# A GpSimd drain ahead of the last 512 rows, and a stricter test on the decays, in a fused attention and MoE kernel

## The chip, the core and the metric

The kernel runs on one core of a Trainium2 chip. Its engines are TensorE (PE; its weight loads are PEld), VectorE (DVE), ScalarE (ACT), GpSimd (POOL) and SyncE (SP), each with an instruction queue of its own; they wait for each other through semaphores. The metric is the device time of one execution in microseconds (us). Before the change three runs took 760.2, 766.49 and 769.64 us, a median of 766.49.

## The reference

Three computations follow one another. The first is a linear attention with a decay for each channel: 4 batches of 8 heads, 768 steps, head size 48.

```python
for t in range(S):
    cur = einsum('bhd,bhe->bhde', u[None] * kt, vt)
    y[:, :, t] = einsum('bhd,bhde->bhe', rt, state + cur)
    state = wt[:, :, :, None] * state + einsum('bhd,bhe->bhde', kt, vt)
```

Its output, 3072 rows of 384, goes through a mixture of eight experts. Each row takes the expert with the largest logit: `out = gate * (max(x @ w1[e], 0) @ w2[e])`, with a hidden width of 1024. The last step is `max(max(x @ v1, x @ v2), x @ v3) @ v_out` with a hidden width of 768. The decays w are drawn as `rand * 0.15 + 0.8`, that is from 0.8 to 0.95.

## The kernel before, in words

The attention works on 24 tiles of 128 rows with scans over the decays. These scans are only good where no decay is extreme, so `flags` marks for every tile and partition whether a decay lay below 0.7 or above 1.4. A tile holds two heads of 48 channels side by side on 128 partitions; the 16 partitions ahead of each are padding, whose decays are set to 1.0 once at the start (`pads`, L649, and two memsets in `attention`). `check_w` counts the good partitions over all 128 with a matmul against ones (L493), compares the count with a limit (L495), and puts the outcome, `badw`, into `ctl`.

The routing sorts rows by expert. GpSimd scatters row numbers into a table in DRAM, gathers them back, and gathers the rows themselves, all by indirect DMAs that it issues from its own queue. The first block (`first_block`) runs the experts on columns of 256 rows. The second block (`second_block`) runs the last step on 512 rows at a time: six turns, j = 0, 2, ..., 10. In a turn `m1` computes the hidden units in six chunks, on TensorE with VectorE and ScalarE behind it, and then `m2` computes the output in four tiles of 128 rows. For each tile ScalarE scales the result into one of four buffers (L1227), and GpSimd issues an indirect DMA that scatters the 128 rows into the output (L1228). In the second block GpSimd has no other work.

Every engine runs its queue in the order in which the code stands; the whole kernel is under a manual schedule. Behind the second block each engine reads `ctl` and branches (L1427, L1428): only where rows remain, or where `badw` is set, the general path runs, with `attention_general` in it. Otherwise GpSimd waits for its DMAs and brings the semaphore counters to the values that the other branch would have left (an INC_SWDGE_SEM, L1428). At the program's end (L1536) SyncE waits for all counters, and every engine drains and meets the others at a barrier twice, with GpSimd clearing the semaphores in between.

Of the kernel before, what the change touches and what calls it, by code (L numbers as in the profile page):

```python
# [15 lines left out]
ALU = mybir.AluOpType  # L16
# [32 lines left out]
def kernel(ctx: ExitStack, tc: tile.TileContext, rkw_t, v_t, vrk, u, modality, w_gate, bias, w1, w2, v1, v2,  # L49
                              v3, v_out, out):  # L50
    nc = tc.nc
    PE, DVE, ACT, POOL, SP = nc.tensor, nc.vector, nc.scalar, nc.gpsimd, nc.sync
    B, NC, _, D, _, HP, _ = rkw_t.shape
# [43 lines left out]
    lgps = lgpool.tile([128, 512], F32, name="lgps")  # L97


    def ct(shape, dt, name):  # L100
        return const.tile(shape, dt, name=name)
# [38 lines left out]
    badw = ct([128, 1], F32, "badw")  # L140
# [214 lines left out]
    def plan(es):  # L355
# [37 lines left out]
        end = t2("end")  # L393
        DVE.tensor_tensor_scan(out=end, data0=zero8, data1=co, initial=cgs, op0=ALU.add, op1=ALU.add)
        checked = check_w()
        next(checked)
        yield "X"
# [88 lines left out]
    def check_w():  # L486

        fl = small.tile([128, 1], F32, tag="fl", name="fl")
        DVE.tensor_reduce(out=fl, in_=flag, axis=AX.XY, op=ALU.max)
        good = small.tile([128, 1], BF16, tag="good", name="good")  # L490
        DVE.tensor_scalar(out=good, in0=fl, scalar1=0.0, scalar2=None, op0=ALU.is_equal)
        yield
        PE.matmul(lgps[:, 272:273], lhsT=ones_bf, rhs=good, start=True, stop=True)  # L493
        yield
        DVE.tensor_scalar(out=badw, in0=lgps[:, 272:273], scalar1=2.0 * D, scalar2=None, op0=ALU.is_lt)  # L495
        yield
        DVE.tensor_copy(ctl[:, 62:63], badw)

# [771 lines left out]
    N = NTILE // 2  # L1270
# [140 lines left out]
    def second_block(vw):  # L1411
        n = 2 * TW
        for j in range(0, N, 2):
            if j + 2 < N:
                xr = ex.fetch(j + 2, n)
            for c in range(KF2):
                ex.m1(c, n, (lambda: vw(V_OPS[5])) if j == 0 else lambda: None)
                if c == MERGE[j > 0] and j + 2 < N:
                    ex.merge(j + 2, xr)
            if j + 2 < N:  # L1420
                ex.x2(xr, j // 2 + 1)
            ex.m2(T[j]["oi"] + T[j + 1]["oi"])

    def rest():

# [36 lines left out]
    with tc.manual_schedule():  # L1462
        wes = ExitStack()
        ex.open_first(wes)
        e = NTILE

        hooks = {(13, "mid"): [chosen, bind(first_load, 0, 0)],
                 (14, "end"): [first_room],
                 (e - 2, "uterm"): [first_x, bind(ex.split_w1, (0, 1, 2))],
                 (e - 2, "late"): [bind(ex.split_w1, (3, 4, 5), "h")],  # L1470
                 (e - 1, "uterm"): [bind(ex.split_w1, (3, 4, 5), "l"), bind(ex.g1, (0,)),
                                    bind(ex.split_w2, (0, 1), W2_FIRST)],
                 (e - 1, "mid"): [bind(ex.split_w2, (2, 3), W2_FIRST)],
                 (e, "mid"): [bind(ex.g1, (1,), rest_of_routing)],
                 (e, "end"): [bind(ex.split_w2, (4, 5), W2_FIRST)]}
        for q in range(1, 7):
            hooks[(13 + q, "mid")] = [bind(first_load, q // 3 if q < 6 else 1, q if q < 3 else q - 3)]
        attention(hooks)
        pools["mm"] = pool(ctx, "mm", 4, space=PSUM)
        wres = pool(ctx, "wres", 1)  # L1480
        vh = [wres.tile([128, KD, F2], F32R, name=f"vh{i}") for i in range(3)]
        vl = [wres.tile([128, KD, F2], F32R, name=f"vl{i}") for i in range(3)]
        voh = wres.tile([128, KF2, DM], F32R, name="voh")
        vol = wres.tile([128, KF2, DM], F32R, name="vol")
        with ExitStack() as es:
            vw = v_stream(pool(es, "stage", 2))
            first_block(vw)
            second_block(vw)
        wes.close()
        rest()  # L1490
# [50 lines left out]
```

## Time and profile before

| what | value |
|---|---|
| median of three runs | 766.49 us |
| the profiled execution | 770.97 us |
| its span, from the first to the last instruction | 769.3 us |
| granted TensorE clock, mean | 0.948 |
| TensorE busy | 720.2 us, 94% |
| VectorE, ScalarE, GpSimd busy | 494.0, 318.7, 363.8 us |

All times of the trace count from the start of the span. The busy times hold the engines' work alone: register, branch, semaphore and DMA-issuing instructions are not counted. A name with a q behind it (POOLq, SPq) is the queue of an engine, where such instructions stand. They are seen by asking for a source line of the kernel.

### The profile page before, as it was taken

What the parts mean: (1) busy time and instruction counts of PE and PEld (TensorE: products, weight loads), DVE (VectorE), ACT (ScalarE), POOL (GpSimd) and SP (SyncE); (2) the same over time, 40 slices, a digit from 0 to 9 for tenths busy, and PEclk for the clock granted to TensorE, in tenths of its full rate; (3) what the DMA queues carried; (4) which work ended last, traced back from release to release, by engine and by line L of the source; (5) the groups of instructions that cost most, each with busy time, mean ns of one, the idle gap of its engine ahead of it and who ended that gap; (6) DMA issues with size and microseconds to landing.
All of it is one profiled execution on the core that took longest, in us unless ns stands there. A gap on an engine that the chain in (4) does not pass through costs nothing.

```text
span 769.3 us, 13303 instructions
## 1 busy us (share of the span) xinstructions
PE 720.2 (94%) x4909; PEld 642.9 (84%) x4910; DVE 494.0 (64%) x929; ACT 318.7 (41%) x698; POOL 363.8 (47%) x388
## 2 busy tenths in 40 slices
PE   6899888889999999999999999999999999999991
PEld 3788767777899989999999987988988889889881
DVE  4899996996786998888888889424143142242320
ACT  5475645554333656566566633211212112122210
POOL 8699868898746667666764435110200101002011
PEclk8699989878599999999999999999999999999996
DMA  9899989993013322122235232020200200001000
GB/s 240 203 249 252 214 173 232 269 273 121 22 50 104 84 65 82 62 65 81 63 118 183 83 124 84 6 77 1 83 0 3 82 0 32 11 0 42 1 21 25
DMA packets 32383, 74.59 MB, mean 97 GB/s; under 512 B 5974, under 2 KB 19062, under 8 KB 32309
## 3 DMA queue, kind: packets, MB, share of 16 engines
q1 hardware_dynamic: 27508, 64.15, 30.5%
q0 software_dynamic: 4800, 9.49, 4.0%
q8 instruction: 41, 0.67, 0.4%
q14 instruction: 34, 0.27, 0.1%
HBM read 87.96 MB, written 14.38 MB: 133 GB/s over the span
## 4 chain that ended last, share of the span: by engine, by line
issue 37%; PE 30%; DVE 12%; DMA 8%; POOL 7%; ACT 2%; POOLq 0%; SPq 0%; DVEq 0%; ACTq 0%
DMA tq<-in_rkw_t_dram 6%; PE mm L1145 6%; PE mm L1144 5%; PE mm L1143 5%; PE yb L805 4%; POOL out_dram L1228 3%; DVE w1l L504 3%; PE mm L775 2%; PE yb L811 2%; DMA vt<-in_v_t_dram 1%; POOL w2l L504 1%; PE tp L788 1%; PE tp L706 1%; PE tp L859 1%; DMA w2r<-in_moe_w_dram 1%
## 5 line engine op out<-in xcount | busy, mean ns | idle before, releaser
L1208 DVE TENSOR_TENSOR w2r<-mm,w2r 128x512 f32<-128x512 f32 x72 | 49.7, 690 | 150.2 <-PE mm L1145 150.1
L1228 POOL DMA_INDIRECT out_dram<-w2r,oi_all x24 | 26.0, 1084 | 250.2 <-ACT w2r L1227 249.6
L1143 PE MATMUL mm<-w1h,vh 128*128 128x512 f32 x324 | 128.2, 396 | 0.9 <-DVE w2r L1208 0.9
L1145 PE MATMUL mm<-w1h,vl 128*128 128x512 f32 x324 | 128.2, 396 | 0.0
L1144 PE MATMUL mm<-w1l,vh 128*128 128x512 f32 x324 | 128.1, 395 | 0.0
L1145 PE MATMUL mm<-hh,w2l 128*128 128x256 f32 x312 | 89.3, 286 | 2.0 <-DVE w2l L504 1.0
L1144 PE MATMUL mm<-hl,w2h 128*128 128x256 f32 x312 | 88.5, 284 | 1.0 <-DVE hl L1157 1.0
L1143 PE MATMUL mm<-hh,w2h 128*128 128x256 f32 x312 | 89.2, 286 | 0.0
L1145 PE MATMUL mm<-xh,w1l 128*128 128x256 f32 x300 | 85.9, 286 | 2.2 <-DVE w1l L504 2.2
L1143 PE MATMUL mm<-xh,w1h 128*128 128x256 f32 x300 | 85.0, 283 | 0.0
L1144 PE MATMUL mm<-xl,w1h 128*128 128x256 f32 x300 | 84.8, 283 | 0.0
L1210 ACT CAST w2h<-w2r 128x512 fp32r<-128x512 f32 x36 | 22.3, 621 | 139.3 <-DVE w2r L1208 139.3
L1143 PEld LDWEIGHTS mm<-w1h,vh 128*128 128x128 f32 x324 | 60.9, 188 | 15.7 <-DVE w2r L1208 1.3
L1145 PEld LDWEIGHTS mm<-w1h,vl 128*128 128x128 f32 x324 | 60.9, 188 | 14.7
L1144 PEld LDWEIGHTS mm<-w1l,vh 128*128 128x128 f32 x324 | 60.9, 188 | 14.4
L504 POOL TENSOR_TENSOR w2l<-w2r,w2h 128x384 fp32r<-128x384 f32 x44 | 49.7, 1136 | 41.6 <-ACT w2h L502 39.1
L504 DVE TENSOR_TENSOR w1l<-w1r,w1h 128x512 fp32r<-128x512 f32 x66 | 51.8, 838 | 23.8 <-ACT w1h L502 23.7
L1145 PEld LDWEIGHTS mm<-hh,w2l 128*128 128x128 f32 x312 | 59.7, 191 | 3.9 <-DVE w2l L504 2.6
L805 PE MATMUL yb<-nat,am 128*128 128x56 f32 x384 | 53.1, 297 | 8.6 <-DVE lh L834 5.0
L1144 PEld LDWEIGHTS mm<-hl,w2h 128*128 128x128 f32 x312 | 59.7, 191 | 1.5 <-DVE hl L1157 1.4
L1145 PEld LDWEIGHTS mm<-xh,w1l 128*128 128x128 f32 x300 | 57.5, 192 | 4.1 <-DVE w1l L504 4.1
L1143 PEld LDWEIGHTS mm<-hh,w2h 128*128 128x128 f32 x312 | 59.8, 192 | 0.0
(252 smaller groups left out, 1728.0 us busy)
## 6 DMA issues: line engine op xcount, KB each, us to landing
w1r<-in_moe_w_dram SPq DMA_DIRECT2D x10, 1536.0 KB, 7.0
w2r<-in_moe_w_dram SPq DMA_DIRECT2D x10, 1536.0 KB
nat<-in_vrk_dram SPq DMA_DIRECT2D x24, 608.0 KB, 10.1
tq<-in_rkw_t_dram SPq DMA_DIRECT2D x46, 288.0 KB, 8.7
stg<-in_moe_w_dram SPq DMA_DIRECT2D x18, 384.0 KB, 3.1
vt<-in_v_t_dram SPq DMA_DIRECT2D x24, 192.0 KB, 6.6
x2t<-raw SPq DMA_DIRECT2D x12, 384.0 KB, 2.3
w1r<-x2t SPq DMA_DIRECT2D x12, 384.0 KB, 3.9
```

The costliest lines, as they stand in the source:

```text
L504: eng.tensor_tensor(out=lo, in0=src, in1=hi.bitcast(F32), op=ALU.subtract)
L706: PE.matmul(ps, lhsT=s["vt"][:, q, :], rhs=wgb[:, q].rearrange("p h e -> p (h e)"), start=(q == 0), stop=(q == KD - 1))
L775: PE.matmul(ps[o][:, p * 128:(p + 1) * 128], lhsT=s["kt"][q, p, :], rhs=s["rt"][q, p, :], start=True, stop=True)
L788: PE.transpose(out=ps[:, p * 128:(p + 1) * 128], in_=s["kt"][:, p, :], identity=ident)
L805: PE.matmul(yb[:, h * DV:(h + 1) * DV], lhsT=s["am"][:, 4 * (h % 2) + h // 2, :], rhs=s["v"][:, h, :], start=(h == 0), stop=(first and h = ...
L811: PE.matmul(yb[:, 2 * p * DV:(2 * p + 2) * DV], lhsT=s["rt"][:, p, :], rhs=sbd[i % 2][:, p, :], start=False, stop=(p == HP - 1))
L1143: PE.matmul(oc, lhsT=wh[:, kk, sl], rhs=xh[:, kk, :], start=first and kk == 0, stop=False)
L1144: PE.matmul(oc, lhsT=wh[:, kk, sl], rhs=xl[:, kk, :], start=False, stop=False)
L1145: PE.matmul(oc, lhsT=wl[:, kk, sl], rhs=xh[:, kk, :], start=False, stop=last and kk == nk - 1)
L1208: DVE.tensor_tensor(out=hv, in0=o, in1=hv, op=ALU.max)
L1210: ACT.copy(self.h2h[:, c, :], hv)
L1228: ins = POOL.indirect_dma_start(out=out[:, :], out_offset=bass.IndirectOffsetOnAxis(ap=ids[q][:, 0:1], axis=0), in_=ob, in_offset=None, bo ...
```

## The change

In `check_w` the limit on the count of good partitions goes from 96 (twice the head size) to 127.5, so that one flagged partition is enough to set `badw`. In `second_block`, in the turn j = 8 (the last but one, as N is 12), GpSimd gets one more instruction behind the four stores of that turn: a drain, with no wait on a semaphore and no semaphore to raise. The turn j = 10 follows. No instruction of any engine changes its place, and none is removed.

```diff
@@ check_w
-        DVE.tensor_scalar(out=badw, in0=lgps[:, 272:273], scalar1=2.0 * D, scalar2=None, op0=ALU.is_lt)
+        DVE.tensor_scalar(out=badw, in0=lgps[:, 272:273], scalar1=127.5, scalar2=None, op0=ALU.is_lt)
@@ second_block
             if j + 2 < N:
                 ex.x2(xr, j // 2 + 1)
             ex.m2(T[j]["oi"] + T[j + 1]["oi"])
+            if j + 4 == N:
+                POOL.drain()
```

## Rows read from the trace of the kernel before

**Rows 1.** The page: span, and TensorE's busy tenths in 40 slices.

```profile
span 769.3 us, 13303 instructions
...
PE   6899888889999999999999999999999999999991
```

**Rows 2.** Windows at the end: length, busy us (instructions) by engine, clock, DMA share, GB/s.

```profile
744.86:753.40 8.54, 8.47 (x49) 8.14 (x47) 0.00 (x0) 1.19 (x3) 2.91 (x3) 1.00 0.21 73
753.40:757.90 4.50, 0.00 (x0) 0.00 (x0) 0.00 (x0) 0.55 (x1) 0.97 (x1) 0.93 0.17 55
757.90:769.30 11.40, 0.00 (x0) 0.00 (x0) 0.00 (x0) 0.00 (x0) 0.00 (x0) 0.50 0.00 1
```

**Rows 3.** GpSimd's timeline: start us, duration us, what, idle time before it.

```profile
703.95 0.97 POOL L1228 DMA_INDIRECT out_dram<-w2r,oi_all  x1 [2.15 <-ACT w2r L1227]
744.86 0.97 POOL L1228 DMA_INDIRECT out_dram<-w2r,oi_all  x1 [39.94 <-ACT w2r L1227]
...
754.22 0.97 POOL L1228 DMA_INDIRECT out_dram<-w2r,oi_all  x1 [2.15 <-ACT w2r L1227]
```

**Rows 4.** The output tensor's instructions: ns min/median/max, idle before, waiters, landing.

```profile
L1228 POOL DMA_INDIRECT out_dram<-w2r,oi_all x24: 971/973/1972, 496.7 to 754.2; - x24
...
who waited for it (us, times):
...
DMA to landing us min/median/max: 2.6/3.0/6.6
```

**Rows 5.** Source line L1428, GpSimd's queue: ns min/median/max, first and last start us.

```profile
L1428 POOLq EVENT_SEMAPHORE  x6: 17/30/100, 757.4 to 757.9; - x6
...
L1428 POOLq INC_SWDGE_SEM  x1: 2188/2188/2188, 758.0 to 758.0; - x1
```

**Rows 6.** Source line L1536, the program's end, by queue; columns as before.

```profile
L1536 SPq EVENT_SEMAPHORE  x14: 17/28/28, 760.1 to 769.2; - x14
...
L1536 POOLq DRAIN  x3: 40/107/8240, 760.2 to 769.0; - x3
L1536 SPq DRAIN  x3: 7/7/13, 760.8 to 768.7; - x3
L1536 DVEq DRAIN  x2: 10/14/17, 746.0 to 768.7; - x2
L1536 PEldq DRAIN  x2: 8/8/8, 754.9 to 768.8; - x2
```

**Rows 7.** Waits of SyncE's queue from 590: us in total, times, longest.

```profile
SPq L1536 <- PEq L1536: 8.3, 2, 7.7
```

**Rows 8.** Source line L1526, the program's start, GpSimd's queue.

```profile
L1526 POOLq INC_SWDGE_SEM  x1: 27/27/27, 0.2 to 0.2; - x1
...
L1526 POOLq DRAIN  x1: 189/189/189, 0.4 to 0.4; - x1
```

**Rows 9.** DMA issues of GpSimd's queue: count, median us to landing.

```profile
order<-idg,places POOLq DMA_INDIRECT x24, 5.0
xin<-xs,oi_all POOLq DMA_INDIRECT x24, 3.4
out_dram<-w2r,oi_all POOLq DMA_INDIRECT x24, 3.0
oi_all<-order,idxm POOLq DMA_INDIRECT x20, 2.5
...
oi_all<-order,idxg POOLq DMA_INDIRECT x4, 5.9
oe<-order,idxx POOLq DMA_INDIRECT x2
xin<-xs,oe POOLq DMA_INDIRECT x2, 2.1
```

**Rows 10.** Source line L495, the test on the count.

```profile
L495 DVE TENSOR_SCALAR badw<-lgps x1: 149/149/149, 227.5 to 227.5; 128x1 f32<-128x1 f32 x1
```

**Rows 11.** The page's groups: busy us, mean ns, idle before.

```profile
L1208 DVE TENSOR_TENSOR w2r<-mm,w2r 128x512 f32<-128x512 f32 x72 | 49.7, 690 | 150.2 <-PE mm L1145 150.1
```

## The prediction

> **What bounds the kernel now.** I read the page first [rows 1]. The span is 769.3 us, and in its 40 slices TensorE's digit is 9 almost without a break. Then the last slice holds a 1. A slice is 19.2 us long, so some 16 us at the end pass without a matmul. No rate of matmuls explains that stretch, so the end has to be read by itself.
>
> The windows cut at the end's events show it [rows 2]. Up to 753.4 TensorE is at work. From 757.9 to 769.3 no engine has any busy time at all: 11.4 us, 1.5% of the span, in which the program only winds up. GpSimd's timeline shows the last work before that: the last four stores of output rows are issued 3.12 us apart, the first at 744.86, the last at 754.22 [rows 3]. A store lands a median of 3.0 us after its issue [rows 4], hence the pause to 757.9.
>
> What fills the 11.4 us is queue work, which the busy columns leave out. It is seen by asking for the source lines of the final branch (L1428) and of the program's end (L1536) [rows 5, 6]. GpSimd's queue does six semaphore waits until 757.9, and the last of them is for the last store. Then one INC_SWDGE_SEM takes 2188 ns (758.0 to 760.2), and then a DRAIN takes 8240 ns (760.2 to 768.4). Two more DRAINs of GpSimd take 107 and 40 ns, the last starts at 769.0, and the span ends. SyncE's queue does its own end waits meanwhile: from 760.1 to 760.9 it goes through them one after the other, and then stands in the closing barrier, which every engine must reach, for 7.7 us [rows 7]. That row names TensorE's queue as the one waited for. TensorE's two drains took 8 ns each, the earlier at 754.9 [rows 6], so the name is that of the last release and not the cause. The only queue with work from 760.9 to 768.4 is GpSimd's, and its work there is that one drain.
>
> **What the drain pays for.** Three rows argue that it pays for the DMAs that GpSimd has issued, one by one. SyncE's queue, which issued the bulk of the traffic through the hardware's own queue, drains in 7 to 13 ns, and VectorE and TensorE in 8 to 17 ns [rows 6]. GpSimd's own drain at the start, before any DMA, took 189 ns [rows 8], and those right behind the long one took 107 and 40 ns, when nothing new had been issued. The long one is also not waiting for data: the semaphores of the stores had all been seen by 757.9, 2.3 us before it began. In between GpSimd had issued 24 + 24 + 24 + 20 + 4 + 2 + 2 = 100 indirect DMAs [rows 9]. 8240 / 100 = 82 ns for each: this is an estimate, and it supposes that the cost is spread evenly over them.
>
> The Trainium skill (VectorE: DVE Perf Modes, The DRAIN you can't avoid) says that the drains that frame a program are a constant of about 12 ns on all five engines. By that rule an added drain costs 12 ns and takes nothing off the end, and the sum below would be zero. The trace agrees for the three other engines shown and disagrees for GpSimd by a factor of several hundred.
>
> **The change, part by part.** *The new constant.* One instruction keeps its place and shape, with 127.5 in place of 96 (149 ns) [rows 10]. It counts the partitions whose decays all lay inside 0.7 to 1.4. The decays are drawn from 0.8 to 0.95, and the 32 padding partitions hold the constant 1.0, set once for each buffer in `pads`. The count is then 128 and the branch falls as before. Cost: 0.
>
> *The added drain.* It stands on GpSimd's queue behind the store issued at 703.95, and carries no wait on a semaphore. The next instruction behind it on that queue belongs to the store at 744.86. In the 39.94 us between, GpSimd is idle [rows 3], and nobody waits for GpSimd there: the row of the stores lists no waiter [rows 4], and ScalarE's reuse of an output buffer waits for landings, not for this queue. The drain covers 96 DMAs: 96 x 82 ns = 7.9 us. Bounds: from 40 ns, the shortest drain of GpSimd [rows 6], up to 8.24 us plus the slowest landing of a store, 6.6 us [rows 4], 14.8 us together. Either end leaves over 25 us of cover, so the cost is 0. Were that cover gone, 7.9 us would stand ahead of the four stores, and all of it would come off the gain.
>
> *The last drain.* It has 4 DMAs left: 4 x 82 = 0.33 us, plus the 0.19 us of an empty one, 0.52 in place of 8.24. But what is late next is SyncE. It reaches the barrier at 760.9, and of its 7.7 us there about 0.2 remain, the way from GpSimd's drain through the release (its end at 768.4, and 760.9 + 7.7 = 768.6). The drain is therefore worth 7.5 us and not 7.7.
>
> *The INC_SWDGE_SEM before it.* It changes the eight counters of GpSimd's DMAs, and SyncE's chain starts only when they have changed (760.1), so it is on the path before and after. Before any DMA the same operation took 27 ns [rows 8]. Bounds: 2188 ns if its length has nothing to do with the finished DMAs, 27 ns if it is all theirs. I take the lower side, since the drain behind it behaves like that: 8 counters x 27 = 0.22 us, the rest of 2188, 1.97 us, spread over 100 DMAs is 20 ns each, and 4 of these are 0.08. That makes 0.30, and the gain 1.9 us.
>
> *The sum.* 7.5 + 1.9 = 9.4 us. Check by the clock of the trace: the increment from 757.96 to 758.26, the drain to 758.8, SyncE's 0.8 us of waits to 759.0, the barrier and the last 0.8 us to 759.9, against 769.3. The profiled execution took 770.97 in all, 1.7 us more than its span, and would take 761.6. It lies 4.5 us above the median of the three runs, 766.49, and the gain does not depend on that. From the median: 766.49 - 9.4 = **757.1 us**. Both ends of the increment: 7.5 (759.0 us) and 9.4.
>
> **Rivals.** *Only the drain shrinks*, the increment keeps its 2.19 us: 759.0 us. For it: the 27 ns row may be another kind of the same operation, since it stands where there was nothing to add. Chance 0.2.
>
> *The last drain is a fixed price* that is due once any DMA of GpSimd has gone since the drain before, as 16 equal checks of half a microsecond (one for each DMA engine of the page) would be. Four stores are then enough to bring it back in full: 766.5 us, no change. The rows above fit that as well, since no drain in this trace stands behind a few DMAs. Against it is only the increment, a second long operation of GpSimd that is nearly free when nothing was issued. Chance 0.16.
>
> *Drains are constants*, and the 8.24 us belong to something else that the row happens to span: the same 766.5 us. No row shows another work there. Chance 0.02. The 12 ns rule of the VectorE page of the Trainium skill would give this time.
>
> The Trainium skill (Perfetto Trace Analysis, Sequencer-only Instruction (DRAIN, etc)) says that the profile shows such an instruction from the moment its waits are met. By that 8.24 us is work and not a wait, and the drain's start right behind the increment agrees. It tells nothing on whether the work is fixed.
>
> *Slower: the new threshold sends the kernel into the general path.* The place is the branch at L1428, the deciding point a count under 127.5, a single partition flagged. Before, up to 32 flagged partitions passed unseen, so the trace cannot show that the count is 128. Only the drawn decays and the pads say so. The price: 16 pairs of heads x 48 columns x 4 VectorE operations over 768 columns, each 1.5 times the 690 ns of 512 columns [rows 11], 1.04 us: 3.2 ms, so some 3,950 us. Chance 0.01.
>
> **How the numbers follow.** Forecast (both shrink) 0.59, drain alone 0.2, no change 0.18 (0.16 and 0.02), general path 0.01, anything else 0.02. The three runs shown lie 760.2 to 769.6, so a median moves by a few microseconds without any cause in the change. Low end: the fastest shown less 9.4, 750.8, rounded to 750.5. High end: the slowest shown less 7.5 is 762.1, and up to 765.5 takes in about two fifths of the no-change case. Inside lie nearly all of 0.79 and 0.4 x 0.18, about 0.8. A change of 2%, 15 us, is what a measurement of this kernel can tell from none. The forecast gain is 1.2%, so within 2% has 0.93, faster by more 0.05 (a gain case with a lucky median), slower 0.02.
>
> **What would show it.** Right: a GpSimd DRAIN of 7 to 9 us starting near 705, the one at the end under 1 us, the increment well under 1 us, SyncE's 7.7 us in the barrier gone, the span's end 6 to 7 us behind the last store's issue in place of 15. Wrong: a second drain of 8 us at the end (fixed price), an increment still near 2.19 us (drain alone), a store at 744.86 that starts late (no cover), or work behind L1428.

## The result and the profile after

The changed kernel takes 754.27 us (median of four runs, 752.42 to 755.5), the kernel before beside it 767.36 us. The ratio is 0.9845 with a 95% interval of 0.9806 to 0.9885, a gain of 1.5%. Timed again later, with more runs, it came to 0.988 (0.9844 to 0.9916).

The page of the profiled execution (754.57 us) now ends in a 6 where a 1 stood.

```profile
span 752.8 us, 13304 instructions
...
PE   6899889888899999999999999999999999999996
```

The windows at the same events as in [rows 2] (length, busy us by engine with instruction counts, clock, DMA share, GB/s):

```profile
738.00:746.51 8.51, 8.48 (x49) 8.16 (x48) 0.00 (x0) 1.16 (x2) 2.92 (x3) 1.00 0.21 74
746.51:750.90 4.39, 0.00 (x0) 0.00 (x0) 0.00 (x0) 0.58 (x1) 0.97 (x1) 0.82 0.16 55
750.90:752.80 1.90, 0.00 (x0) 0.00 (x0) 0.00 (x0) 0.00 (x0) 0.00 (x0) 0.50 0.01 4
```

Before, 11.40 us passed between the landing of the last store and the end; now 1.90 us do. The two stretches ahead of it are nearly as long as they were (8.51 against 8.54 us, 4.39 against 4.50). What shrank in the last one is on GpSimd's queue. First the branch line (L1428 before, [rows 5], L1430 now, since the change adds two lines), with ns min/median/max and first and last start:

```profile
L1430 POOLq EVENT_SEMAPHORE  x6: 17/30/43, 750.4 to 750.9; - x6
...
L1430 POOLq INC_SWDGE_SEM  x1: 268/268/268, 751.0 to 751.0; - x1
```

Then the program's end, L1538 now, against [rows 6]:

```profile
L1538 SPq EVENT_SEMAPHORE  x14: 17/28/28, 751.2 to 752.8; - x14
...
L1538 POOLq DRAIN  x3: 46/107/386, 751.3 to 752.5; - x3
L1538 SPq DRAIN  x3: 7/7/7, 751.9 to 752.2; - x3
```

The drain went from 8240 to 386 ns, the increment from 2188 to 268 ns (the increment is the INC_SWDGE_SEM). SyncE's queue hardly stands in the barrier any more; its row of waits, against [rows 7], holds 0.5 us for the second meeting and 0.2 for the one that took 7.7:

```profile
SPq L1538 <- PEq L1538: 0.7, 2, 0.5
```

The added drain shows under its own source line:

```profile
L1424 POOLq DRAIN  x1: 9120/9120/9120, 696.9 to 696.9; - x1
```

GpSimd's timeline around it (start, duration, idle time before) shows what it costs:

```profile
697.10 0.97 POOL L1228 DMA_INDIRECT out_dram<-w2r,oi_all  x1 [2.15 <-ACT w2r L1227]
738.00 0.97 POOL L1228 DMA_INDIRECT out_dram<-w2r,oi_all  x1 [39.94 <-ACT w2r L1227]
...
747.37 0.97 POOL L1228 DMA_INDIRECT out_dram<-w2r,oi_all  x1 [2.15 <-ACT w2r L1227]
```

The drain's record starts at 696.9, ahead of the store in front of it, and it ends at 706.0. From that store's end (698.07) it is 7.9 us. The next store finds GpSimd idle for 39.94 us ahead of it, exactly as in [rows 3]: the cover held.

From the last store's issue to the end it was 769.3 - 754.2 = 15.1 us and is 752.8 - 747.4 = 5.4 us: 9.6 us less. But the last store itself stands 6.8 us earlier. The added drain has no hand in that, as the difference is there at the first store already, 200 us ahead of the drain: it was issued at 496.7 before [rows 4] and now at 489.9.

```profile
L1228 POOL DMA_INDIRECT out_dram<-w2r,oi_all x24: 971/972/1974, 489.9 to 747.4; - x24
```

The windows of the attention stage and of what follows, of the kernel before:

```profile
0.00:215.00 215.00, 187.95 (x1626) 159.89 (x1628) 178.03 (x396) 117.28 (x309) 179.84 (x206) 0.84 0.79 201
215.00:690.00 475.00, 468.89 (x2978) 427.51 (x2977) 300.40 (x513) 187.54 (x368) 175.78 (x175) 1.00 0.20 62
```

and of the changed kernel:

```profile
0.00:215.00 215.00, 186.36 (x1699) 158.84 (x1701) 191.02 (x438) 118.77 (x313) 182.83 (x209) 0.91 0.77 201
215.00:690.00 475.00, 467.78 (x2944) 425.75 (x2943) 294.54 (x474) 187.50 (x367) 177.03 (x172) 1.00 0.20 63
```

The clock granted to TensorE is 1.00 in both from 215 us on, and 0.84 against 0.91 before that. With two levels, 2.4 and 1.2 GHz, 0.84 means 0.16 x 2 x 215 = 69 us at the lower one, 0.91 means 39 us. In this stage TensorE is idle for 27 and 29 of the 215 us. How long its clock stands at the lower level differs between executions, and the first store moves with it: in the trace of the limit alone, below, the clock of this stage is 0.84 and the first store comes at 497.7, in that of the drain alone 0.86 and 497.4, in the later one of the changed kernel 0.87 and 492.5. What lowers the clock is not shown. The runs of the kernel before spread over 9 us, the runs of the changed kernel in the later measurement over 10. The four runs of the first measurement lay in the lower half of that.

### The profile page after: what moved, and what is told of

It reads as the page before. It is cut to its first block, busy times and chain, and to the rows that moved or that the text cites. A ratio compares the mean times of both kernels' runs of the same rounds, so it can differ in the third digit from the quotient of the medians.

```text
span 752.8 us, 13304 instructions
## 1 busy us (share of the span) xinstructions
PE 710.6 (94%) x4909; PEld 633.4 (84%) x4910; DVE 498.0 (66%) x929; ACT 317.6 (42%) x698; POOL 366.7 (49%) x388
## 4 chain that ended last, share of the span: by engine, by line
issue 39%; DVE 11%; PE 10%; POOL 6%; DMA 1%; ACT 1%; POOLq 0%; DVEq 0%; ACTq 0%; SPq 0%
PE mm L1145 4%; PE mm L1144 3%; PE mm L1143 3%; POOL out_dram L1228 3%; DVE w1l L504 3%; POOL w2l L504 1%; DVE t L541 1%; DVE w2l L504 1%; DVE hl L1157 1%; DVE ya L528 1%; DMA w2r<-in_moe_w_dram 1%; DVE ya L532 1%; POOL vl L559 1%; DVE ya L536 1%; DVE ya L545 1%
## 5 line engine op out<-in xcount | busy, mean ns | idle before, releaser
L805 PE MATMUL yb<-nat,am 128*128 128x56 f32 x384 | 50.0, 286 | 10.8 <-DVE lh L834 6.8
```

The source lines that it names most:

```text
L805: PE.matmul(yb[:, h * DV:(h + 1) * DV], lhsT=s["am"][:, 4 * (h % 2) + h // 2, :], rhs=s["v"][:, h, :], start=(h == 0), stop=(first and h = ...
```

## Experiments

**Each part alone.** The edits are the two halves of the diff. First the limit alone:

```diff
-        DVE.tensor_scalar(out=badw, in0=lgps[:, 272:273], scalar1=2.0 * D, scalar2=None, op0=ALU.is_lt)
+        DVE.tensor_scalar(out=badw, in0=lgps[:, 272:273], scalar1=127.5, scalar2=None, op0=ALU.is_lt)
```

> The kernel before with the new limit of 127.5 alone, no added drain. Theory (all of the gain is the end's bookkeeping of GpSimd's DMAs, the rest of the 13 us is the scatter of the granted clock in the attention stage): no change, ratio 1.000 within 0.006, the end as before with a last drain of 8.24 us and an increment of 2.19 us, 15 us from the last store's issue to the end. Rival (the 3.5 us of the measured gain that the end does not explain belong to the changed program): a ratio near 0.995, with the last store's issue earlier and the end still 15 us behind it.

Measured: ratio 0.999 (0.9966 to 1.0015). Its end is that of the kernel before: an increment of 2188 ns, a last drain of 8240 ns, 14.9 us from the last store's issue to the end. The limit does nothing to the time that this measurement can tell, and the general path stays untouched. The test itself (L495) took 1491 ns in this trace, against 149 before [rows 10] and 151 in the changed kernel; why is open.

Then the drain alone:

```diff
             ex.m2(T[j]["oi"] + T[j + 1]["oi"])
+            if j + 4 == N:
+                POOL.drain()
```

> The kernel before with the added drain alone, the old limit of 96. Theory: the whole gain of the end, 9.6 us, so a ratio of 0.9875 against the runs beside it, last drain 0.39 us, increment 0.27 us, 5.4 us from the last store's issue to the end. Rival (the drain also makes the earlier stages faster): a ratio of 0.983, that is 13 us.

Measured: ratio 0.9875 (0.984 to 0.991), and at the program's end

```profile
L1538 POOLq DRAIN  x3: 46/107/386, 759.0 to 760.3; - x3
```

The gain belongs to the drain, and its size is that of the end. The rival's 0.983 lies outside the interval, by little. In this trace the end is 5.7 us behind the last store's issue and not 5.4, as it is in the later trace of the changed kernel: the gain of the end is 9.3 to 9.6 us.

**The drain earlier: is the price for each DMA?** With the new limit, the drain stands behind the first turn's stores.

```diff
-            if j + 4 == N:
+            if j == 0:
                 POOL.drain()
```

> The added drain stands behind the stores of the first turn (j = 0) in place of the last but one, so 80 indirect DMAs lie ahead of it and 20 behind. Theory (82 ns for each DMA since the last drain): the added drain pays 80 x 82 = 6.5 us and runs 7.6 us from its record's start, a little over one store's 0.97 us more; the last drain is 0.06 + 20 x 81.8 ns = 1.7 us, the increment 0.19 + 20 x 20 ns = 0.59 us, 6.7 us from the last store's issue to the end. Rival (a price by steps: few DMAs cost nothing, many cost it all): a last drain of 0.4 us or of 8.2 us.

Its last drain and its increment, by source line:

```profile
L1538 POOLq DRAIN  x3: 46/107/1692, 752.9 to 755.1; - x3
```
```profile
L1430 POOLq INC_SWDGE_SEM  x1: 588/588/588, 752.2 to 752.2; - x1
```

1692 and 588 ns against 1.7 and 0.59 us expected; the end was 7.0 us behind the last store's issue against 6.7. With 4, 20 and 100 DMAs since the last drain the price grows with their number, and not in steps. The added drain's record lasted 7815 ns, 7.6 us expected.

**Two drains: does it matter what the DMAs moved?**

```diff
         n = 2 * TW
+        POOL.drain()
         for j in range(0, N, 2):
```

> The change, with one more drain at the start of the second block, when 76 DMAs of the routing and of the rows have gone and no store. Theory (the same price for each DMA, whatever it moved): the first drain 76 x 82 ns = 6.2 us, about 7 with what it still waits for; the second covers 20 stores, 1.7 us, but cannot end before the store ahead of it has landed, so 3.5 to 4.5 us from its record's start; the end as with the change, 0.39 and 0.27 us. Rival (the price goes by bytes, so the stores carry it): the first drain short, 1 to 3 us, the second near 6 us.

Both added drains by source line (the first at the start of the second block, the second where the change has it):

```profile
L1413 POOLq DRAIN  x1: 7353/7353/7353, 439.0 to 439.0; - x1
```
```profile
L1425 POOLq DRAIN  x1: 3682/3682/3682, 697.7 to 697.7; - x1
```

The first record holds GpSimd's instruction in front of it too, which ran from 438.99 to 440.01. From there to the drain's end it is 6.3 us, and 76 DMAs at 82 ns are 6.2. The rival was badly put: 26 of the 76 are gathers of rows as long as those that the stores write, so a price by bytes would give the first drain a little over half of the 7.9 us, some 4.5 us and not 1 to 3. The 6.3 us speak against that as well; the gathers of two words a row, further on, settle it. GpSimd still converts weights in the first turn of the second block (L559), so only from the second turn on does it have no other work there.

The 20 stores should cost 1.7 us. Their drain ends 3.5 us behind the issue of the store in front of it (697.89), 0.8 us later than the price alone gives. The median store lands 3.0 us after its issue [rows 4], so this fits a drain that also waits for the last DMA ahead of it to land. In the other runs the price outlasts a landing, so they cannot tell.

**No cover.** The drain moves behind the first store of the last turn.

```diff
                 done(q)
+                if q in drain_behind:
+                    POOL.drain()
...
-            ex.m2(T[j]["oi"] + T[j + 1]["oi"])
+            ex.m2(T[j]["oi"] + T[j + 1]["oi"], (0,) if j + 2 == N else ())
```

> The added drain moved to a place without cover: behind the first of the four stores of the last turn (97 DMAs ahead of it, 3 behind), with the new limit. Theory (a drain holds GpSimd's queue for 82 ns per DMA): it runs to 7.9 us past the end of that store's 0.97 us, so the second to fourth store, due 3.12 us apart, queue up behind it and go 1.3 us apart; the last store is issued 2.3 us later than with the change, the end behind it is the same 5.4 us. Against the kernel before -7.2 us, a ratio of 0.9905. Rival (the bookkeeping runs beside the queue and holds nothing up): stores 3.12 us apart as ever, a ratio of 0.9875 as with the drain alone.

GpSimd's timeline, and the drain:

```profile
742.88 0.97 POOL L1228 DMA_INDIRECT out_dram<-w2r,oi_all  x1 [39.94 <-ACT w2r L1227]
752.72 0.97 POOL L1228 DMA_INDIRECT out_dram<-w2r,oi_all  x1 [8.87 <-ACT w2r L1227]
753.99 0.97 POOL L1228 DMA_INDIRECT out_dram<-w2r,oi_all  x1 [0.30 <-issue]
755.27 0.97 POOL L1228 DMA_INDIRECT out_dram<-w2r,oi_all  x1 [0.31 <-issue]
```
```profile
L1247 POOLq DRAIN  x1: 9203/9203/9203, 742.6 to 742.6; - x1
```

The second store waits 8.87 us and the others follow 1.27 us apart. The wait is put down to ScalarE, which had filled the buffer by 745.7; the queue was held by the drain, which the busy columns do not show. Without it the last store would come at 742.88 + 3 x 3.12 = 752.24. It comes at 755.27, 3.0 us late, where 2.3 had been expected: the drain ends at 751.8, but the first store behind it starts only 0.9 us later. The end is 4.6 us behind the last store and not 5.4. The ratio is 0.9917 (0.9882 to 0.9951), against 0.9905 expected and 0.9875 if the queue had not been held. The interval leaves out the rival, by little; the rows leave it out clearly, with 8.87 us of idle queue ahead of the second store in place of 2.15.

**More DMAs in place of a drain.** No drain is added; 20 gathers into a tile that nobody reads follow the stores of the turn j = 8.

```diff
+    oj = ct([128, 20, 2], I32, "oj")
...
             ex.m2(T[j]["oi"] + T[j + 1]["oi"])
+            if j + 4 == N:
+                for q in range(20):
+                    ex.gather_ids(oj[:, q, :], idxm[:, q:q + 1])
```

> No added drain, the new limit, and 20 more indirect gathers of GpSimd (128 rows of two words each, into a tile that nobody reads) in its idle stretch behind the stores of the last but one turn, so 120 DMAs stand before the last drain. Theory (82 and 20 ns for each DMA): last drain 0.06 + 120 x 81.8 ns = 9.9 us, increment 0.19 + 120 x 20 ns = 2.6 us, 17.1 us from the last store's issue to the end. Rival (a price that stops growing, or one for bytes: these move 1 KB each): 8.2 and 2.2 us as before, 15 us.

This expectation failed, and so did its rival:

```profile
L1540 POOLq DRAIN  x3: 40/107/1217, 747.9 to 749.7; - x3
```
```profile
L1432 POOLq INC_SWDGE_SEM  x1: 468/468/468, 747.4 to 747.4; - x1
```

By the prices found so far (drain 0.06 us + 81.8 ns, increment 0.19 us + 20 ns for each DMA) both rows say 14 DMAs, where 120 had been issued. 106 were written off before the end, without any added drain. The next run has the same number of gathers with fewer rows:

```diff
-                    ex.gather_ids(oj[:, q, :], idxm[:, q:q + 1])
+                    ex.gather_ids(oj[0:16, q, :], idxm[0:16, q:q + 1])
```

> The same 20 more gathers, each of 16 rows in place of 128. Theory (the price is for each DMA, whatever its number of rows): last drain 9.9 us, increment 2.6 us. Rival (the price is for each row or descriptor): 8.24 + 20 x 82/8 ns = 8.4 us, increment near 2.2 us.

```profile
L1540 POOLq DRAIN  x3: 46/107/9868, 754.3 to 764.7; - x3
```
```profile
L1432 POOLq INC_SWDGE_SEM  x1: 2588/2588/2588, 751.6 to 751.6; - x1
```

9868 and 2588 ns against 9.9 and 2.6 expected: with small DMAs the line goes on, and a DMA of 16 rows costs as much as one of 128, be it a store or a gather of two words a row. So it is the rows, or what goes with them, and not the number of DMAs, that decide when GpSimd writes off by itself. Two more numbers of full gathers, 10 and 16 (`range(10)`, `range(16)`, and a tile of that size):

> No added drain, the new limit, 10 more gathers of 128 rows in the idle stretch, 110 DMAs before the last drain. With 20 more the last drain took 1.22 us and the increment 0.47 us, as for 14 DMAs, so 106 had been written off somewhere on the way. Theory (GpSimd writes finished DMAs off by itself only when its room for descriptors runs out, between 100 and 120 full DMAs): if room is left at 110, the last drain 0.06 + 110 x 81.8 ns = 9.1 us, the increment 2.4 us; if not, a drain of 1 us or less. Rival (a gather with many rows frees others' entries as it goes): a drain between these, near 4 to 5 us. The weights lie shifted by 80 or 96 bytes: turns of 49.57 us if an offset of 32 in 64 bytes matters.

```profile
L1540 POOLq DRAIN  x3: 40/107/9057, 760.0 to 769.6; - x3
```
```profile
L1432 POOLq INC_SWDGE_SEM  x1: 2388/2388/2388, 757.6 to 757.6; - x1
```

> The same with 16 more gathers, 116 DMAs. Theory: the room has run out by then, as at 120, and the last drain covers some 10 DMAs, 0.9 us, the increment 0.4 us. Rival (it runs out between 116 and 120): 9.5 and 2.5 us. The weights lie shifted by 128 bytes, the same offset in 64 bytes as in the change: turns of 50.27 us.

```profile
L1540 POOLq DRAIN  x3: 40/107/890, 752.6 to 754.1; - x3
```
```profile
L1432 POOLq INC_SWDGE_SEM  x1: 388/388/388, 752.2 to 752.2; - x1
```

110 full DMAs are paid in full at the end, 9.1 and 2.4 us as expected. Of 116 only 10 are left, again 106 gone. In that kernel the second store of the last turn, the 114th DMA, is late:

```profile
738.93 1.03 POOL L1229 DMA_INDIRECT out_dram<-w2r,oi_all  x1 [18.64 <-ACT w2r L1228]
743.53 1.01 POOL L1229 DMA_INDIRECT out_dram<-w2r,oi_all  x1 [3.57 <-issue]
```

Due 3.12 us behind the first, it comes 4.60 us behind, with nothing that it waited for. It fits a queue that stops to make room at about 113 full DMAs, but the 3.57 us of idle queue are less than the 8.7 us that 106 DMAs would cost a drain. With 20 gathers no such stop is seen at the 114th DMA. Where and at what price the 106 are written off stays open.

**A side effect: where the weights lie.** The two kernels with a tile of 160 bytes had turns (from a turn's first store to the next one's) of 49.57 us in place of 50.27. As built, that tile moves the weights of the second block by 160 bytes, and tiles of the attention stage too. Tried on the changed kernel:

```diff
+    shift = ct([128, 40], I32, "shift")
+    POOL.memset(shift, 0)
```

> The changed kernel with an unused tile of 160 bytes per partition (set once by one memset at the start), which moves the weights of the second block by 160 bytes and leaves all other large tiles where they were. In the two kernels with 20 more gathers, which have a tile of that size, the first stores of two following turns lay 49.57 us apart, in all others 50.27. Theory (the place of these weights does it): 49.57 us in this kernel too, so 6 x 0.7 = 4.2 us less than the change, a ratio of 0.982 against the kernel before. Rival (the gathers or the missing drain did it): 50.27 us, a ratio of 0.9875.

The turns were 49.57 us, with the drain in place and no gathers, so the tile does it; of the large tiles that the second block works on, it moves the weights alone. The ratio was 0.9849 (0.98 to 0.9897), which holds both theories. Hence the change and the shifted kernel side by side:

> The change as it stands, timed on the same chip as the next kernel. Theory: the end's 9.6 us, a ratio of 0.9875; the 0.9845 of the first measurement held some 2 us of the attention stage's scatter. Turns of 50.27 us.

> The change with the weights of the second block moved by 160 bytes, beside it. Theory (turns of 49.57 us are worth 4.2 us): a ratio 0.0055 below that of the change beside it, near 0.982. Rival (the turns gain, but something else gives it back, since the first measurement gave 0.9849): the same ratio as the change, 0.985 to 0.9875.

Measured: 0.988 (0.9844 to 0.9916) for the change, 0.982 (0.977 to 0.9869) for the shifted kernel, 755.75 and 751.59 us. The difference of 0.006 is about the 0.0055 expected, but the intervals overlap. The traces show a source for it. GpSimd's idle time before a turn's first store, in the change:

```profile
640.05 1.39 POOL L1228 DMA_INDIRECT out_dram<-w2r,oi_all  x1 [39.94 <-ACT w2r L1227]
```

and shifted:

```profile
636.98 1.39 POOL L1230 DMA_INDIRECT out_dram<-w2r,oi_all  x1 [39.23 <-ACT w2r L1229]
```

The three matmuls of `mm3` between 594 and 690 us (busy us, mean ns), in the change:

```profile
L1145 PE MATMUL mm<-w1h,vl 128*128 128x512 f32 x108 | 42.7, 396 | 0.0
L1143 PE MATMUL mm<-w1h,vh 128*128 128x512 f32 x108 | 42.7, 395 | 0.0
L1144 PE MATMUL mm<-w1l,vh 128*128 128x512 f32 x108 | 42.7, 395 | 0.0
```

and shifted:

```profile
L1147 PE MATMUL mm<-w1h,vl 128*128 128x512 f32 x108 | 42.6, 394 | 0.0
L1146 PE MATMUL mm<-w1l,vh 128*128 128x512 f32 x108 | 42.3, 392 | 0.0
L1145 PE MATMUL mm<-w1h,vh 128*128 128x512 f32 x108 | 41.9, 388 | 0.0
```

The matmuls are 2 to 7 ns shorter, at the same granted clock of 1.00. Which offset it takes is open, and so is the reason. The guess of the expectations, an offset of 32 within 64 bytes, fell: a shift of 96 bytes, with 10 gathers, gave turns of 50.3 to 50.5 us, like the shift of 128 bytes with 16. Turns vary that much without any shift: with the drain behind the first turn they were 50.5 us, not the 50.27 that the expectation names for all other kernels. The 751.59 us of the shifted kernel are the lowest median of all kernels here.

## Why the prediction was right

- **Where the end goes.** Right. 11.4 us without any busy engine were queue work of GpSimd, and the long drain was the last thing that anybody waited for.
- **82 ns for each DMA.** Right, and now with a slope of its own: last drains of 304 (3 DMAs), 386 (4; 376 with two drains), 1692 (20), 8240 (100), 9057 (110) and 9868 ns (120, 20 of them small) lie within 0.02 us of 0.06 us + 81.8 ns for each. That the cost is spread evenly was only supposed in the prediction; its rows fitted a fixed price as well. That rival, 766.5 us, is refuted by the 386 ns alone.
- **The increment.** Right, though it was the least supported term: 0.30 us was forecast and 0.268 measured. 248, 268, 588, 2188, 2388 and 2588 ns are 188 + 20 ns for each DMA to the nanosecond. The split of 20 ns for each DMA was forecast; the constant came out at 0.19 in place of 0.22 us. That it came so near is luck: the 27 ns that the prediction took eight times belong to another kind of the instruction, which as built names no counter at all, as the rival had suspected. "Only the drain shrinks" falls all the same, with the 268 ns.
- **The next wait.** Right: SyncE's chain of waits, 0.8 us behind the increment, now sets the end, and 0.2 us of its barrier wait are left.
- **Cover.** Right: 7.9 us forecast and measured, under 39.94 us of idle queue. Without it the drain holds the stores up, by 3.0 us where three stores were left to run behind each other.
- **The limit.** Right: 0.999.
- **The sum.** 9.4 us forecast, 9.3 to 9.6 measured in the traces, and 0.9875 for the drain alone. The forecast of 757.1 us lies 2.8 us above the 754.27 measured. The limit alone and the drain alone leave nothing of it to the change (0.999 and 0.9875), and timed again the change gives 0.988, some 9 us. The two traces differ by 6.8 us ahead of the first store, with a clock of 0.84 and 0.91 in the attention stage. So the excess of the first measurement is put down to that stage's scatter.
- **The sign.** "6 to 7 us behind the last store's issue" was loose: the working itself gave 759.9 - 754.2 = 5.7, and 5.4 was measured (5.7 in two later traces).

The 12 ns of the Trainium skill (VectorE: DVE Perf Modes, The DRAIN you can't avoid) are near what VectorE, SyncE, ScalarE and TensorE show at the end of the changed kernel too (7 to 17 ns). GpSimd's drain after indirect DMAs is another thing, 0.3 to 9.9 us in these runs. The prediction also took a drain's record for work alone, and there the traces disagree: the added drain's record begins 0.2 us ahead of the store in front of it and holds that store as well. The 8.24 us at the end were work all the same, as the increment in front had ended when they began and 100 DMAs lie on the line.

## What to carry to other kernels

Look past the last busy instruction: the queue rows of the last source lines tell what the end waits for, and busy columns do not. Where GpSimd issues many indirect DMAs, a price for each (here 82 ns) is owed until a drain pays it, unless so many rows go by that it is written off on the way (here at 116 DMAs of 128 rows); a drain in a stretch in which GpSimd's queue has nothing to do moves the debt from the end to where it is covered. Put it late enough to leave few DMAs behind it, and never ahead of work that is due.

## What the runs showed of the hardware that was not expected

- GpSimd writes off finished DMAs by itself once enough rows have gone: not at 110 DMAs of 128 rows, but at 116 and 120, and each time 106 of them. The last drain then covers the rest only (890 and 1217 ns).
- With the weights 160 bytes further on, the 128x512 matmuls were 2 to 7 ns shorter at the same granted clock, 0.7 us in a turn of 50.27, in all four traces with such a tile. Shifts of 96 and 128 bytes did not do it.
- A drain's record can start before the instruction ahead of it on GpSimd has started (696.9 against 697.10 for a store), so its length holds that instruction too, here 0.97 us.
